# Order of the first loads, and of the first K chunks, in a gated mix of two linear-attention blocks

## The chip, the cores and the metric

The kernel runs on one core of a Trainium2 chip. The metric is device time in microseconds (us), the median of three timed runs. A core has TensorE (PE) for matmuls, VectorE (DVE), ScalarE (ACT), GpSimd (POOL) and SyncE (SP), each with an instruction queue of its own, and 16 DMA engines, which take the transfers that SP and ACT issue.

## The reference

x has 2048 rows of 640, there are two blocks A and B with 32 heads of 20, and only A's x is used.

```python
g = sigmoid((x * gate_w).sum(-1))
for each block:
    q, k, v = split(x @ wqkv)               # 640 -> 3 x 640, by heads
    phi = lambda t: where(t > 0, t + 1, exp(t)) + 1e-6
    pq, pk = phi(q), phi(k)
    kv = pk^T v ; z = sum over rows of pk   # by head
    o = (pq kv) / (pq z + 1e-6)
    y = o @ wo
out = g * a + (1 - g) * b
```

## The kernel before

x is held twice: as rows in `xn` (128 partitions, 16 chunks of 128 rows, 640) and transposed in `xT` (128 partitions, 5 column blocks, 2048). The first four row chunks of `xT` are made by PE: `x_transpose` transposes the five 128x128 blocks of a chunk into a PSUM tile `xt` and VectorE copies them out, in one piece or in two (blocks 0 and 1, then 2 to 4; `cuts`). The other twelve chunks come by transposing DMAs from HBM, issued by SP (L135).

A K chunk is x @ wk for 128 rows: ten matmuls of 320 columns, five column blocks c by two halves (`k_mm`, L207), summed in one of four PSUM slots of two banks each. `k_done` then calls `phi`: an exp on ACT (L197), a `tensor_scalar` on VectorE (min with 1, plus epsilon, L200) and a `scalar_tensor_tensor` on VectorE (x + 1, max, L204), which writes `pk`. Q products have weights as the stationary operand and 512 rows of xT as the moving one (L256, L267).

The program starts like this. SP and ACT issue the first loads: four chunks of x (160 KB each, `load_x`, L117) and the five row blocks of wkA (160 KB each, `load_wk`, L120). After them SP issues wqA (800 KB, L131) and the transposing loads. PE runs seven warm-up matmuls on constants (L164) and then `k_first`, whose order is written out by hand under `manual_schedule`: every engine takes its instructions in the order in which they are written. `k_first` handles chunks 0 to 3. Before, chunks 0 and 1 are transposed, their blocks c = 0 and 1 are multiplied, chunk 2 is transposed, block 2 of chunks 0 and 1 follows, then blocks 0 to 2 of chunk 2, the transposes of chunk 3, blocks 3 and 4 of chunks 0, 1 and 2 with `k_done` after each, and at last chunk 3 as a whole. Then come Q products and further K chunks, then block A's sums, block B, and the output products.

DMAs signal landing on eight semaphores in turn. A ninth transfer is issued only when the first one on its semaphore has landed; before, that is wqA.

Of the kernel before, what the change touches and what calls it, by code (L numbers as in the profile page):

```python
# [8 lines left out]
P = 128  # L9
# [7 lines left out]
DT = D // P  # L17
# [3 lines left out]
HB = 512  # L21
# [12 lines left out]
def kernel(  # L34
# [11 lines left out]
    nc = tc.nc  # L46
# [13 lines left out]
    def ps_raw(name, slot=None):  # L60

        if slot is None:
            slot = turn[0]
            turn[0] = (slot + 1) % 4
        return psum.tile([P, 4 * HB], BF16, tag=f"ps{slot}", name=name)

    def ps(name, slot=None):

        return ps_raw(name, slot).bitcast(FP32).rearrange("p (b n) -> p b n", b=2)

    xT = persist.tile([P, DT, S], BF16, name="xT")
# [44 lines left out]
    def load_x(eng, lo, hi):  # L116
        eng.dma_start(out=xn[:, lo:hi, :], in_=xb0[:, lo:hi, :])  # L117

    def load_wk(eng, lo, hi):
        eng.dma_start(out=wk[0][:, lo:hi, :], in_=wq_dram[0][:, lo:hi, D:2 * D])  # L120

    load_x(nc.sync, 0, 1)
    load_x(nc.scalar, 1, 2)
    load_wk(nc.sync, 0, 1)
    load_wk(nc.scalar, 1, 2)
    load_wk(nc.sync, 2, 3)
    load_x(nc.scalar, 2, 3)
    load_wk(nc.sync, 3, DT)
    load_x(nc.scalar, 3, 4)
    wq[0] = wpool.tile([P, DT, D], BF16, tag="wq", name="wqA")  # L130
    nc.sync.dma_start(out=wq[0][:], in_=wq_dram[0][:, :, 0:D])  # L131
    gcol = persist.tile([P, DT], BF16, name="gcol")
    for n in range(1, NB):
        for c in range(DT):
            nc.sync.dma_start_transpose(  # L135
                out=xT[:, c, n * HB:(n + 1) * HB], in_=x2[n * HB:(n + 1) * HB, c * P:(c + 1) * P]
# [4 lines left out]
    for r in range(4):  # L141
# [3 lines left out]
        out=spread[:].rearrange("p (h t) -> p h t", t=TW), in_=I4[:, :, None].to_broadcast([P, H, TW])  # L145
    )
    nc.gpsimd.memset(maskE[:], 1.0)
    for sign, base in ((1, 0), (-1, Dh - 1)):
        nc.gpsimd.affine_select(
            out=maskE[:], in_=maskE[:], pattern=[[-sign * Dh, WB[0] // Dh], [0, Dh]],  # L150
# [3 lines left out]
    for sign, base in ((1, 0), (-1, TW - 1)):  # L154
        nc.gpsimd.affine_select(
            out=headE[:], in_=headE[:], pattern=[[-sign * TW, H]],
# [25 lines left out]
            nc.scalar.activation(out=ge[b][:], in_=pt[:, 1, :], func=ACT.Exp, scale=(-1.0, 1.0)[b])  # L182
            nc.vector.tensor_scalar(ge[b][:], ge[b][:], 1.0, 1e30, op0=ALU.add, op1=ALU.min)

    def x_transpose(i, slot, eng, cuts=(0, DT)):
        pt = ps_raw("xt", slot)
        for c in range(DT):
            nc.tensor.transpose(out=pt[:, c * P:(c + 1) * P], in_=xn[:, i, c * P:(c + 1) * P], identity=ident[:])
        copy = nc.scalar.copy if eng == "act" else nc.vector.tensor_copy
        src = pt[:, 0:D].rearrange("p (c n) -> p c n", c=DT)  # L190
        for lo, hi in zip(cuts, cuts[1:]):
            copy(out=xT[:, lo:hi, i * P:(i + 1) * P], in_=src[:, lo:hi])  # L192

    def phi(dst, src, n, lifted=False):

        e = work.tile([P, 2, n], BF16, tag="e", name="e", bufs=3)
        nc.scalar.activation(out=e[:], in_=src, func=ACT.Exp)  # L197
        if lifted:
            nc.scalar.activation(out=dst, in_=src, func=ACT.Identity, bias=lift[:])
        nc.vector.tensor_scalar(e[:], e[:], 1.0, EPS, op0=ALU.min, op1=ALU.add)  # L200
        if lifted:
            nc.vector.tensor_tensor(out=dst, in0=dst, in1=e[:], op=ALU.max)
            return
        nc.vector.scalar_tensor_tensor(out=dst, in0=src, scalar=1.0 + EPS, in1=e[:], op0=ALU.add, op1=ALU.max)  # L204

    def k_mm(b, i, c, pt, hf):
        nc.tensor.matmul(  # L207
            pt[:, hf, 0:HF], lhsT=xT[:, c, i * P:(i + 1) * P], rhs=wk[b][:, c, hf * HF:(hf + 1) * HF],
            start=(c == 0), stop=(c == DT - 1),
        )  # L210

    def k_done(b, i, pt):
        phi(pk[:, i, :].rearrange("p (b n) -> p b n", b=2), pt[:, :, 0:HF], HF)

    def k_chunk(b, i, slot=None):
        pt = ps(f"k{'AB'[b]}", slot)
        for hf in range(2):
            for c in range(DT):
                k_mm(b, i, c, pt, hf)
        k_done(b, i, pt)  # L220

    def k_first():

        pts = [ps("kA", (2 + i) % 4) for i in (0, 1)]

        def part(i, cs):
            for c in cs:
                for hf in range(2):
                    k_mm(0, i, c, pts[i], hf)

        for i in range(2):
            x_transpose(i, i, "dve", (0, 2, DT))
        for i in range(2):
            part(i, (0, 1))
        x_transpose(2, 0, "dve", (0, 2, DT))
        for i in range(2):
            part(i, (2,))
        pts.append(ps("kA", 1))
        part(2, (0, 1, 2))
        x_transpose(3, 0, "dve")  # L240
        for i in range(3):
            part(i, (3, 4))
            k_done(0, i, pts[i])
        k_chunk(0, 3, 0)

    def mixed(t, m):
# [426 lines left out]
    with tc.manual_schedule():  # L673
        k_first()
# [11 lines left out]
    for n in range(1, NB):  # L686
        nc.sync.dma_start(
            out=xn[:, n * CB:(n + 1) * CB, :], in_=x2[n * HB:(n + 1) * HB, :].rearrange("(q p) d -> p q d", p=P)
# [8 lines left out]
    def bank(pool, name, n=1):  # L697
        return pool.tile([P, HB] if n == 1 else [P, n, HB], FP32, tag=name, name=name)

    with tc.manual_schedule():  # L700
# [30 lines left out]
        part = [slice(n * RB, (n + 1) * RB) for n in range(4)]  # L731
# [17 lines left out]
        with late_pool("single") as single:  # L749
# [6 lines left out]
            pts = [bank(single, f"s4{hf}")[:, 0:HF] for hf in range(2)]  # L756
# [20 lines left out]
        later = {2: (2, (1, 2)), 3: (2, (4,)), 4: (3, (2, 4))}  # L777
# [55 lines left out]
```

## Time and profile before

| what | value |
|---|---|
| timed runs | 189.77, 189.83 and 190.37 us; median 189.83 |
| profiled execution, its span (first to last instruction) | 188.1 us; the median of the runs is 1.7 us above it |
| busy: PE, DVE, ACT, POOL | 182.7 us (97%), 150.3 (80%), 75.0 (40%), 2.8 (2%) |
| granted TensorE clock | 1.000 |
| DMA | 15.63 MB, mean 83 GB/s; 319 to 387 GB/s from 3 to 8 us |
| first transposes; first k matmul; first q matmul | at 3.90, 4.77 and 11.72 us |

The profile is of one execution, and its times count from the start of its span. It gives no time of that execution other than the span. A timeline row names its start, how long the group lasted, the engine, the line, the operation with the tile written and the tiles read, the number of instructions, and in brackets the idle time before it and what ended that. A matmul's duration is that of one result; the next one starts earlier, so rates are read from starts. Rows with PEld are weight loads, those with ACTq and SPq are issues from these queues. "DMA to landing" is the time from issue until the last part of a transfer has signalled.

### The profile page before, as it was taken

The page shows a single profiled execution, that of the slowest core. Times are in us where ns is not written, and L with a number is a line of the kernel's source. Part 1 is how long each engine was busy: PE and PEld are TensorE (multiplying, and loading weights), DVE is VectorE, ACT ScalarE, POOL GpSimd, SP SyncE. Part 2 cuts the span into 40 slices and gives each one's busy share as a digit, 9 for nine tenths or more (in the row PEclk, how much of TensorE's full clock was granted, in tenths as well). Part 3 has the DMA queues.
Part 4 walks back from the last instruction along what each step waited for, and adds up shares of the span by engine and source line. Part 5 has one row for each costly group of instructions (what it writes and reads, how often), then busy time and mean ns, then how long its engine had stood idle before and what let it go on. Part 6 is the DMA issues. An engine that isn't in the chain of part 4 may idle for free.

```text
span 188.1 us, 3574 instructions
## 1 busy us (share of the span) xinstructions
PE 182.7 (97%) x1460; PEld 123.5 (66%) x1465; DVE 150.3 (80%) x244; ACT 75.0 (40%) x106; POOL 2.8 (2%) x17
## 2 busy tenths in 40 slices
PE   8899999999999999999999999999999999999992
PEld 3566657755577677877765555576778776777772
DVE  1378968899998999799889997739699989787553
ACT  2055446457942501367674577422401611111110
POOL 6000000000000000000000000000000000000000
PEclk9999999999999999999999999999999999999999
DMA  5975447992140000011115000000543003211222
GB/s 184 320 124 94 105 84 250 360 249 87 16 164 0 3 0 0 3 33 33 54 44 189 2 0 0 3 0 0 178 112 62 3 3 112 97 70 56 87 71 71
DMA packets 19802, 15.63 MB, mean 83 GB/s; under 512 B 9546, under 2 KB 19658, under 8 KB 19786
## 3 DMA queue, kind: packets, MB, share of 16 engines
q1 hardware_dynamic: 18922, 14.59, 29.0%
q10 hardware_dynamic: 864, 0.82, 1.3%
q8 instruction: 11, 0.18, 0.4%
q14 instruction: 5, 0.04, 0.1%
HBM read 10.00 MB, written 3.44 MB: 71 GB/s over the span
## 4 chain that ended last, share of the span: by engine, by line
PE 93%; DMA 3%; DVE 1%; ACTq 0%; issue 0%; ACT 0%; DVEq 0%
PE gs L325 16%; PE kB L207 12%; PE qB L256 11%; PE kA L207 11%; PE qA L256 7%; PE ox L563 6%; PE oy L563 5%; PE oz L563 5%; PE qA L267 5%; DMA xn<-in_A_x_dram 3%; PE ow L563 3%; PE gB L298 2%; PE gA L298 2%; DVE osb L568 1%; PE mA L456 1%; PE mid L417 1%
## 5 line engine op out<-in xcount | busy, mean ns | idle before, releaser
L207 PEld LDWEIGHTS <-xT 128*128 128x128 bf16 x320 | 31.0, 98 | 12.4 <-DVE xT L192 0.5
L200 DVE TENSOR_SCALAR e<-e 128x640 bf16<-128x640 bf16 (+1 forms) x52 | 18.7, 360 | 6.3 <-ACT e L197 5.7
L207 PE MATMUL kB<-wkB,xT 128*128 128x320 bf16 x160 | 23.0, 299 | 0.0
L207 PE MATMUL kA<-wkA,xT 128*128 128x320 bf16 x160 | 22.6, 299 | 0.1
L256 PE MATMUL qB<-xT,wqB 128*128 128x512 bf16 x98 | 21.7, 379 | 0.1
L197 ACT ACTIVATE e<-kB 128x640 bf16<-128x640 f32 x16 | 11.3, 704 | 18.8 <-PE kB L207 17.5
L256 PEld LDWEIGHTS <-wqB 128*128 128x128 bf16 x100 | 11.7, 117 | 9.8 <-issue 0.2
L197 ACT ACTIVATE e<-kA 128x640 bf16<-128x640 f32 x16 | 11.0, 704 | 13.3 <-PE kA L207 13.3
L204 DVE SCALAR_TENSOR_TENSOR pk<-kA,e 128x640 bf16<-128x640 f32 x16 | 13.2, 825 | 1.7
L204 DVE SCALAR_TENSOR_TENSOR pk<-kB,e 128x640 bf16<-128x640 f32 x16 | 13.2, 825 | 1.7
L197 ACT ACTIVATE e<-qA 128x1024 bf16<-128x1024 f32 x10 | 10.2, 1023 | 9.3 <-PE qA L267 3.7
L197 ACT ACTIVATE e<-qB 128x1024 bf16<-128x1024 f32 x10 | 10.2, 1023 | 8.7 <-PE qB L256 8.4
L256 PE MATMUL qA<-xT,wqA 128*128 128x512 bf16 x59 | 13.2, 379 | 0.1
L607 ACT COPY u<-ox 128x320 f32<-128x320 f32 x8 | 3.4, 425 | 21.9 <-PE ox L563 21.9
L325 PEld LDWEIGHTS <-S 128*128 128x128 bf16 x96 | 9.4, 98 | 3.6
L325 PEld LDWEIGHTS <-xn 128*128 128x128 bf16 x96 | 9.1, 98 | 4.0 <-issue 0.4
L256 PEld LDWEIGHTS <-wqA 128*128 128x128 bf16 x60 | 7.0, 117 | 5.8
L563 PEld LDWEIGHTS <-xT 128*128 128x128 bf16 x85 | 8.0, 98 | 3.1 <-DVE xT L502 0.2
L591 ACT COPY p1s<-ox 128x320 f32<-128x320 f32 x8 | 3.4, 426 | 16.6 <-PE ox L563 16.6
L563 PEld LDWEIGHTS <-pqTA 128*128 128x128 bf16 x85 | 7.9, 98 | 2.9 <-issue 0.2
L563 PEld LDWEIGHTS <-pqTB 128*128 128x128 bf16 x80 | 7.8, 98 | 3.0
L325 PE MATMUL gs<-pk,xn 128*128 128x320 bf16 x64 | 9.4, 300 | 0.0
(124 smaller groups left out, 285.2 us busy)
## 6 DMA issues: line engine op xcount, KB each, us to landing
out_dram<-osb SPq DMA_DIRECT2D x14, 160.0 KB, 1.8
xn<-in_A_x_dram SPq DMA_DIRECT2D x3, 640.0 KB, 6.8
wqA<-in_A_wqkv_dram SPq DMA_DIRECT2D x1, 800.0 KB, 7.3
wvA<-in_A_wqkv_dram SPq DMA_DIRECT2D x1, 800.0 KB, 11.8
wkB<-in_B_wqkv_dram SPq DMA_DIRECT2D x1, 800.0 KB, 6.3
wqB<-in_B_wqkv_dram SPq DMA_DIRECT2D x1, 800.0 KB, 4.8
MA<-ma_dram SPq DMA_DIRECT2D x1, 800.0 KB, 4.3
wvB<-in_B_wqkv_dram SPq DMA_DIRECT2D x1, 800.0 KB, 5.7
```

The source lines that it names most:

```text
L197: nc.scalar.activation(out=e[:], in_=src, func=ACT.Exp)
L200: nc.vector.tensor_scalar(e[:], e[:], 1.0, EPS, op0=ALU.min, op1=ALU.add)
L204: nc.vector.scalar_tensor_tensor(out=dst, in0=src, scalar=1.0 + EPS, in1=e[:], op0=ALU.add, op1=ALU.max)
L207: nc.tensor.matmul(pt[:, hf, 0:HF], lhsT=xT[:, c, i * P:(i + 1) * P], rhs=wk[b][:, c, hf * HF:(hf + 1) * HF], start=(c == 0), stop=(c == D ...
L256: nc.tensor.matmul(pt[:, u, :], lhsT=mixed(wq[b][:, c, :], m), rhs=xT[:, c, n * HB:(n + 1) * HB], start=(c == 0), stop=(c == DT - 1),)
L267: nc.tensor.matmul(pt[:, u, :], lhsT=mixed(wq[b][:, c, :], m + u), rhs=xT[:, c, n * HB:(n + 1) * HB], start=(c == 0), stop=(c == DT - 1),)
L298: nc.tensor.matmul(pt[:, hf, 0:HF], lhsT=xn[:, i, c * P:(c + 1) * P], rhs=pk[:, i, hf * HF:(hf + 1) * HF], start=(i == 0), stop=(i == ST - 1),
L325: nc.tensor.matmul(pt[:, n, 0:HF], lhsT=left[:, i, n * P:(n + 1) * P], rhs=right[:, i, :], start=(first and i == 0), stop=(i == hc - 1), s ...
L417: nc.tensor.matmul(pt[:KG, hf, j * KG:(j + 1) * KG], lhsT=wv[b][:, c, (4 * hf + j) * KG:(4 * hf + j + 1) * KG], rhs=GT[hf][:, c, j * KG:(j ...
L563: nc.tensor.matmul(dst, lhsT=left[:, c, r0:r0 + P], rhs=right[:, c, :], start=(first and c == 0), stop=(c == DT - 1), skip_group_check=not ...
L591: nc.scalar.copy(out=self.p1s[:], in_=self.at("x"))
L607: nc.scalar.copy(out=self.u2[:], in_=self.at("x"))
```

## The change

The first loads are issued in another order and from other queues. Before, SP: x0, wk0, wk2, wk3 and wk4 in one; ACT: x1, wk1, x2, x3. After, SP: x0, x1, wk2, wk4, x3; ACT: wk0, wk1, wk3, x2. There are nine transfers instead of eight, so x3 is now the one that waits for an earlier landing (wk0's) on the shared semaphore.

In `k_first`, chunks 0 and 1 are transposed as before; then blocks 0 to 3 are multiplied for both chunks in turn; then chunk 2 is transposed; then block 4 of chunks 0 and 1 follows, with `k_done` of each; then chunk 2 with all its blocks; then the transposes of chunk 3, `k_done` of chunk 2, and chunk 3. Chunk 2's copy to xT is one instruction instead of two, and the transposes of chunks 2 and 3 write the two halves of one PSUM tile. On VectorE the copy of chunk 3 now stands behind the `phi` instructions of chunks 0 and 1 and ahead of those of chunk 2; before it stood ahead of all of them.

```diff
     load_x(nc.sync, 0, 1)
-    load_x(nc.scalar, 1, 2)
-    load_wk(nc.sync, 0, 1)
+    load_wk(nc.scalar, 0, 1)
+    load_x(nc.sync, 1, 2)
     load_wk(nc.scalar, 1, 2)
     load_wk(nc.sync, 2, 3)
+    load_wk(nc.scalar, 3, 4)
+    load_wk(nc.sync, 4, DT)
     load_x(nc.scalar, 2, 3)
-    load_wk(nc.sync, 3, DT)
-    load_x(nc.scalar, 3, 4)
+    load_x(nc.sync, 3, 4)
...
-    def x_transpose(i, slot, eng, cuts=(0, DT)):
-        pt = ps_raw("xt", slot)
+    def x_transpose(i, pt, cuts=(0, DT)):
...
         for i in range(2):
-            x_transpose(i, i, "dve", (0, 2, DT))
+            x_transpose(i, ps_raw("xt", i), (0, 2, DT))
+        for c in range(DT - 1):
+            for i in range(2):
+                part(i, (c,))
+        later = ps_raw("xt", 0)
+        x_transpose(2, later[:, 0:2 * HB])
         for i in range(2):
-            part(i, (0, 1))
-        x_transpose(2, 0, "dve", (0, 2, DT))
-        for i in range(2):
-            part(i, (2,))
+            part(i, (DT - 1,))
+            k_done(0, i, pts[i])
         pts.append(ps("kA", 1))
-        part(2, (0, 1, 2))
-        x_transpose(3, 0, "dve")
-        for i in range(3):
-            part(i, (3, 4))
-            k_done(0, i, pts[i])
+        part(2, range(DT))
+        x_transpose(3, later[:, 2 * HB:])
+        k_done(0, 2, pts[2])
         k_chunk(0, 3, 0)
```

More of the change, by code (lines that the diff above doesn't have):

```diff
@@ L183, in gate_pass @@
             nc.vector.tensor_scalar(ge[b][:], ge[b][:], 1.0, 1e30, op0=ALU.add, op1=ALU.min)
-    def x_transpose(i, slot, eng, cuts=(0, DT)):
-        pt = ps_raw("xt", slot)
+    def x_transpose(i, pt, cuts=(0, DT)):
         for c in range(DT):
             nc.tensor.transpose(out=pt[:, c * P:(c + 1) * P], in_=xn[:, i, c * P:(c + 1) * P], identity=ident[:])
-        copy = nc.scalar.copy if eng == "act" else nc.vector.tensor_copy
         src = pt[:, 0:D].rearrange("p (c n) -> p c n", c=DT)
         for lo, hi in zip(cuts, cuts[1:]):
-            copy(out=xT[:, lo:hi, i * P:(i + 1) * P], in_=src[:, lo:hi])
+            nc.vector.tensor_copy(out=xT[:, lo:hi, i * P:(i + 1) * P], in_=src[:, lo:hi])
     def phi(dst, src, n, lifted=False):
```

## Prediction

> **What bounds the kernel now.** I read the chain of waits first, for the engine that sets the end.
>
> ```profile
> PE 93%; DMA 3%; DVE 1%; ACTq 0%; issue 0%; ACT 0%; DVEq 0%
> ```
>
> The chain is PE from end to end, with one piece of DMA. Busy time by stretches then tells whether a delay could be taken back: from 12 to 182 us PE is busy for 169.7 of 170 us (3.95 of 4.00, 5.95 of 6.00, 17.95 of 18.00, and so on), and after 182 us come only the last products, additions and stores. So the start of the first q product is the clock of everything behind it: what the change adds or saves ahead of it comes out at the end one for one.
>
> Next the chain inside the first 15 us:
>
> ```profile
> 1.73 5.02 DMA xn<-in_A_x_dram
> 6.75 0.05 issue
> 6.79 0.45 PE xt L188 x5
> 7.25 1.37 PE kA L207 x10
> 8.62 0.28 PE xt L188 x5
> 8.90 2.99 PE kA L207 x22
> ```
>
> The DMA piece is the third x chunk: issued by ACT at 1.73, landed at 6.75, its transposes at 6.79. The PE timeline shows the hole, and the rates I shall need:
>
> ```profile
> 0.84 3.06 PE L164 MATMUL warm<-const-bfloat16-1.0 128*128 128x512 bf16 x7 [0.84 <-PEq L817]
> 3.90 0.73 PE L188 MATMUL xt<-ident,xn 128*128 128x128 bf16 x10
> 4.77 1.25 PE L207 MATMUL kA<-wkA,xT 128*128 128x320 bf16 x8
> 6.79 0.45 PE L188 MATMUL xt<-ident,xn 128*128 128x128 bf16 x5 [0.77 <-DMA xn<-in_A_x_dram]
> 8.74 3.15 PE L207 MATMUL kA<-wkA,xT 128*128 128x320 bf16 x22
> 11.72 4.48 PE L267 MATMUL qA<-xT,wqA 128*128 128x512 bf16 x19
> ```
>
> A k matmul takes (11.72-8.74)/22 = 0.1355 us of PE's time, its result 0.30 us; a transpose takes 0.28/5 = 0.056. From 3.90 to 11.72 lie 20 transposes (1.12) and 40 k matmuls (5.42), 6.54 us of work in 7.82: 1.28 us idle. Two holes make it: 0.31 before 4.77 (the first copy of xT) and 6.79-(4.77+8x0.1355) = 0.94 before 6.79. That 0.94 is all there is to win from the loads, and not all can be won: wqA is issued at 4.07 and lands 7.3 us later, at 11.4, where q starts its weight load at 11.59.
>
> Last, VectorE, which the change reorders:
>
> ```profile
> 4.39 1.02 DVE L192 COPY xT<-xt 128x256 bf16<-128x256 bf16 x4 [2.91 <-PE xt L188]
> 7.28 0.56 DVE L192 COPY xT<-xt 128x256 bf16<-128x256 bf16 x2 [1.87 <-PE xt L188]
> 8.94 0.49 DVE L192 COPY xT<-xt 128x640 bf16<-128x640 bf16 x1 [1.10 <-PE xt L188]
> 10.22 0.33 DVE L200 TENSOR_SCALAR e<-e 128x640 bf16<-128x640 bf16 x1 [0.79 <-ACT e L197]
> 10.67 0.82 DVE L204 SCALAR_TENSOR_TENSOR pk<-kA,e 128x640 bf16<-128x640 f32 x1
> 11.41 0.32 DVE L200 TENSOR_SCALAR e<-e 128x640 bf16<-128x640 bf16 x1
> 11.83 0.82 DVE L204 SCALAR_TENSOR_TENSOR pk<-kA,e 128x640 bf16<-128x640 f32 x1
> 12.57 0.32 DVE L200 TENSOR_SCALAR e<-e 128x640 bf16<-128x640 bf16 x1
> ```
>
> All xT copies stand ahead of the first phi. The copy of the fourth chunk (8.94) is done at 9.43, under matmuls that do not need it. Each phi then holds VectorE for 1.16 us (10.22, 11.41, 12.57).
>
> **Part 1, the loads.** Issue to landing of each in the DMA view: SP's first (x0) 3.0 and ACT's first (x1) 3.2, so 3.8 and 4.0; the second ones (wk0, wk1) 3.5 and 3.7, so 4.75 and 4.95; the third ones (wk2, x2) 4.8 and 5.0, so 6.5 and 6.75; the fourth ones (wk rows 3 and 4 as one 320 KB transfer, x3) 5.7 and 5.4, so 7.8 and 7.6. From 3 to 8 us the DMA share is 0.95 to 1.08 with 319 to 387 GB/s, so it is place in the queue that sets a landing, not the queue's name. I give the new order the old landings place by place: x0 3.8, wk0 4.0, x1 4.75, wk1 4.95, wk2 6.5, wk3 6.75, x2 7.6, wk4 7.4 to 7.8. x3 is now SP's fifth and the ninth transfer on eight semaphores; its issue waits for wk0's landing (4.0), as wqA's waited for x1's, so wqA and the fifteen transposing loads go out some 0.4 us later (one SP issue, 0.39 to 0.44). That is hidden: wqA would land near 11.8 and is wanted, below, at 13.3; the first transposed block is wanted at 16.04 plus the shift. If PE came early it would not be hidden.
>
> **Part 2, the start on PE.** The transposes of x0 still run at 3.90 to 4.18 (the warm-up matmuls end there anyway). x1 was there at 4.0; now PE waits until 4.75+0.05 = 4.80: 0.62 idle. Its transposes end at 5.08, chunk 0 has two matmuls to 5.35, and chunk 1 needs the first copy of x1: transposes to copy 0.49 (3.90 to 4.39), copy 0.28, copy to weight load 0.07, to matmul 0.03, so 5.67: 0.32 idle. Then c0 of chunk 1 and c1 of both, six matmuls, to 6.48, c2 from wk2 at 6.55 (0.07 idle) to 7.09, c3 to 7.63 (wk3 is there). x2 at 7.65: transposes to S = 7.93. The hole of 0.94 is gone, but 0.62+0.32+0.07+0.02 = 1.03 us of new ones replace it and the old 0.31.
>
> **Part 3, the end of the k start, counted from S.** c4 for chunks 0 and 1: four matmuls to S+0.54. Chunk 2 needs all of x2's copy, now one piece (0.49): copy from S+0.21, weight load S+0.77, matmul S+0.80, so 0.26 idle. Ten matmuls end at S+2.155, x3's transposes at S+2.435. Before, this copy lay under fourteen matmuls and more. Now the next instruction on PE is chunk 3, which needs it, and on VectorE it is issued behind the phis of chunks 0 and 1. Those run so: the last c4 matmul of chunk 0 ends at S+0.435, ACT's exp at S+0.465 (as 9.45 to 9.48 before), tensor_scalar 0.74 later at S+1.205 (9.48 to 10.22), scalar_tensor_tensor 0.45 later at S+1.655 (10.22 to 10.67), next tensor_scalar 0.74 later at S+2.395, its partner 0.42 later at S+2.815, and the copy 0.74 later at S+3.555. It ends at S+4.045, chunk 3 starts at S+4.145: PE idle for 1.71 us. Were the copy taken as soon as the transposes allow (S+2.155+0.49 = S+2.645), chunk 3 would start at S+3.235 and PE idle 0.80; that is the low bound of this term, 0.91 less. I take 1.71: VectorE's rows of before stand in program order, and the third tensor_scalar came at 12.57 although the three exps were done at 9.48+1.90 = 11.38.
> [...]
>
> **The sum.** Idle between the first transposes and q: before 0.31+0.94 = 1.25; after 1.03+0.26+1.71 = 3.00. The work is the same 40 matmuls and 20 transposes, and one VectorE copy less costs nothing (its chunk is off the path except for the 0.26 counted). Difference +1.75; by absolute times, S+5.50 = 13.43 against 11.72, +1.71. I take +1.7. Against the profiled execution that is a span of 189.8 for 188.1; the median of the runs, 189.83, is 1.7 above the span and I keep that distance: 191.5 us.
>
> **The bounds.** Low: if x1, wk2 and x2 all land as early as the matmuls can use them, PE sets S alone: 5.85 (where the first eight matmuls end before) + 8x0.1355 + 0.28 = 7.2, which makes the difference +1.0; with late loads but the low bound of the copy, 0.91 less, it is +0.8: 190.6. Both at once are a rival. High: one load late by what a third landing lost against a second (1.75 from second to third, 0.95 from first to second, so 0.8), or timed runs of before in which the 0.94 hole was small: +2.6, so 192.5.
>
> **The rivals.**
> *The weights of q decide in both kernels.* wqA landed 0.2 us ahead of need; landings here vary from 3.0 to 7.4 us. If in timed executions it lands after 13.4, that is 9.3 us after issue and not 7.3, q starts there in either kernel and the late copy costs nothing; only the 0.4 of the later issue is left: 189.8 to 190.2. Against it: in the trace PE starts q without a wait, and the runs agree within 0.6 us. 4%.
> *The loads win and the copy passes.* With S at 7.2 and the copy of x3 taken as soon as it is ready, idle is 0.31+0.26+0.80 = 1.37 against 1.25: 189.9, no change. For it: the 0.94 hole does go, and part of a load's lag may be chance. Against it: x1 is now second on its queue, and the copy must overtake two phis on VectorE. 3%. Even this is no gain: PE has nothing to do between x3's transposes and chunk 3, so a faster kernel would need something that I do not see; 2% for that.
> *The clock falls in the new holes.* The warm-up's 512-column matmuls start 0.42 apart, q's later 0.22 apart; after the 0.94 us hole of before the k matmuls kept 0.137, so that hole cost no clock. One of 1.71 us is not shown. If it halved the rate for as long as the warm-up took (3.06 us), half of that, 1.5 us, comes on top: 193.0. 4%.
> [...]
>
> **How the numbers follow.** The forecast, slower by about 1.7 us, has 87%, the rivals 4, 3 and 4%, the unseen gain 2%. A measurement of this kernel can tell 0.3%, 0.57 us, from no change. Slower by more: 0.91 (forecast and clock); within: 0.07; faster: 0.02. The range 190.6 to 192.5 leaves out the rivals (11%), the unseen gain and the ends of the forecast.
>
> **What would show it.** Right: PE idle ahead of x1's transposes until about 4.8, no hole before x2's; VectorE with two tensor_scalar and scalar_tensor_tensor pairs ahead of the last 128x640 copy; chunk 3 waiting on that copy for 1.5 to 1.9 us; q near 13.4; PE closed after that. Wrong: that copy starting within 0.5 us of x3's transposes, q's first matmul waiting for wqA, or any k matmul at 0.27 instead of 0.135.

## The result, and the profile after

The changed kernel takes 191.09 us (median of 6 runs, 190.85 to 191.50), the kernel before 189.96 (6 runs, 189.61 to 190.56): ratio 1.0057, 95% interval 1.0038 to 1.0076, so 1.1 us slower. A second comparison gave 1.0071 (1.0041 to 1.0101). The forecast was 191.5, slower.

The profiled execution took 191.50 us with a span of 189.6, so 1.9 us lie around the span; it was the slowest of the six. Its PE timeline answers to the one shown of before:

```profile
3.80 1.49 PE L188 MATMUL xt<-ident,xn 128*128 128x128 bf16 x10
5.08 3.10 PE L206 MATMUL kA<-wkA,xT 128*128 128x320 bf16 x16
8.02 0.44 PE L188 MATMUL xt<-ident,xn 128*128 128x128 bf16 x5
8.30 2.28 PE L206 MATMUL kA<-wkA,xT 128*128 128x320 bf16 x14
10.42 0.44 PE L188 MATMUL xt<-ident,xn 128*128 128x128 bf16 x5
12.39 1.53 PE L206 MATMUL kA<-wkA,xT 128*128 128x320 bf16 x10 [1.53 <-DVE xT L191]
13.76 4.48 PE L267 MATMUL qA<-xT,wqA 128*128 128x512 bf16 x20
```

The hole ahead of chunk 2's transposes is gone; a larger one stands ahead of chunk 3, from 10.42+0.28 = 10.70 to 12.39, and its releaser is the copy on L191. q starts at 13.76 for 11.72. VectorE's timeline shows why that copy is late:

```profile
8.50 0.49 DVE L191 COPY xT<-xt 128x640 bf16<-128x640 bf16 x1 [2.61 <-PE xt L188]
9.51 0.33 DVE L199 TENSOR_SCALAR e<-e 128x640 bf16<-128x640 bf16 x1 [0.52 <-ACT e L196]
9.95 0.82 DVE L203 SCALAR_TENSOR_TENSOR pk<-kA,e 128x640 bf16<-128x640 f32 x1
10.69 0.32 DVE L199 TENSOR_SCALAR e<-e 128x640 bf16<-128x640 bf16 x1
11.11 0.82 DVE L203 SCALAR_TENSOR_TENSOR pk<-kA,e 128x640 bf16<-128x640 f32 x1
11.85 0.48 DVE L191 COPY xT<-xt 128x640 bf16<-128x640 bf16 x1
```

The transposes of chunk 3 began at 10.42; with 0.49 from transposes to copy, it could have started at 10.91. It starts at 11.85, with no idle time before it: the two phis ahead of it filled VectorE. The chain of waits now runs through ACT's exp and these phis (pieces in order of time):

```profile
8.46 0.29 PE kA L206 x2
8.77 0.71 ACT e L196
10.78 0.24 DVE e L199
11.11 0.82 DVE pk L203
11.94 0.41 DVE xT L191
12.39 1.53 PE kA L206 x10
```

Yet q is 2.04 us later and the span only 1.5 longer. The rest is at the other end of the program, in the DMA view of the last stores, before and then after:

```profile
out_dram<-osb ACTq DMA_DIRECT2D x2, 80.0 KB, 2.0
out_dram<-osb SPq DMA_DIRECT2D x2, 80.0 KB, 1.8
```

```profile
out_dram<-osb ACTq DMA_DIRECT2D x2, 80.0 KB, 1.6
out_dram<-osb SPq DMA_DIRECT2D x2, 80.0 KB, 1.6
```

The last VectorE additions, before and then after:

```profile
184.50 0.61 DVE L568 TENSOR_TENSOR osb<-oz,u 128x160 bf16<-128x160 f32 x2
```

```profile
186.54 0.61 DVE L568 TENSOR_TENSOR osb<-oz,u 128x160 bf16<-128x160 f32 x2
```

From q's start to these additions both kernels take the same (184.50-11.72 = 172.78, 186.54-13.76 = 172.78), but the last four stores land sooner, and from q's start to the end of the span it is 175.8 instead of 176.4.

### The profile page after: what moved, and what is told of

Read it like the earlier page. It is cut to its first block, busy times and chain, and to the rows that moved or that the text cites. A ratio compares the mean times of both kernels' runs of the same rounds, so it can differ in the third digit from the quotient of the medians.

```text
span 189.6 us, 3578 instructions
## 1 busy us (share of the span) xinstructions
PE 184.3 (97%) x1465; PEld 124.1 (65%) x1465; DVE 150.1 (79%) x243; ACT 75.1 (40%) x106; POOL 2.8 (1%) x17
## 4 chain that ended last, share of the span: by engine, by line
PE 93%; DVE 3%; DMA 2%; ACT 1%; issue 0%; SPq 0%; DVEq 0%; ACTq 0%
PE gs L325 16%; PE kB L206 11%; PE qB L256 11%; PE kA L206 11%; PE qA L256 7%; PE ox L563 6%; PE oy L563 5%; PE oz L563 5%; PE qA L267 5%; PE ow L563 3%; PE gB L298 2%; PE gA L298 2%; DMA xn<-in_A_x_dram 2%; DVE osb L568 1%; DVE pk L203 1%; PE mA L456 1%
## 5 line engine op out<-in xcount | busy, mean ns | idle before, releaser
L206 PE MATMUL kA<-wkA,xT 128*128 128x320 bf16 x160 | 23.5, 305 | 1.6 <-DVE xT L191 1.5
L203 DVE SCALAR_TENSOR_TENSOR pqTB<-qB,e 128x1024 bf16<-128x1024 f32 x7 | 8.6, 1225 | 1.1 <-PE qB L256 0.5
```

The costliest lines, as they stand in the source:

```text
L206: nc.tensor.matmul(pt[:, hf, 0:HF], lhsT=xT[:, c, i * P:(i + 1) * P], rhs=wk[b][:, c, hf * HF:(hf + 1) * HF], start=(c == 0), stop=(c == D ...
```

## The experiments

Theory 1: VectorE's order and the uncovered copies make the kernel slower. Theory 2: the order of the loads does. Theory 3: a TensorE clock that rises later does. Ratios are to the kernel before, run beside each on the same chip; its medians there were 190.17 to 190.26 us.

**Phis behind the copy (e1).** Loads and PE order as in the changed kernel:

```diff
         for i in range(2):
             part(i, (DT - 1,))
-            k_done(0, i, pts[i])
...
         x_transpose(3, later[:, 2 * HB:])
-        k_done(0, 2, pts[2])
+        for i in range(3):
+            k_done(0, i, pts[i])
```

> The changed kernel with the phis of chunks 0 and 1 issued behind the copy of chunk 3 on VectorE; loads and PE order unchanged. If the copy's place behind two phis costs 0.9 us (theory 1), the copy starts about 0.5 us after x3's transposes begin, PE idles 0.7 to 0.8 us before chunk 3 instead of 1.5, and the time falls to about 190.2 us. If the later landing of x1 makes the loss (theory 2), or a TensorE clock that rises later (theory 3), it stays near 191.1.

190.07 us, 0.9994 (0.9976 to 1.0013). The loss is gone.

```profile
9.76 0.44 PE L188 MATMUL xt<-ident,xn 128*128 128x128 bf16 x5
10.79 1.53 PE L206 MATMUL kA<-wkA,xT 128*128 128x320 bf16 x10 [0.59 <-DVE xT L191]
```

PE idles from 10.04 to 10.79, 0.75 us against 1.69: the place behind two phis costs 0.94 us. What is left is the wait for the copy itself, with no other work for PE under it.

**Both transposes together (e2).** `x_transpose(3, ...)` directly behind `x_transpose(2, ...)`.

> The changed kernel with the transposes and the copy of chunk 3 right behind those of chunk 2, so ahead of block 4 and of the phis on PE and on VectorE; loads unchanged. Theory 1: both idle stretches behind S (0.26 and 1.5 to 1.7 us) are gone, q starts 1.8 us earlier unless wqA's landing near 11.4 us holds it: 189.2 to 189.7 us, so 0.3 to 0.7 below the kernel before. Theory 2: x1's lateness stays in full and the time is 190.5 or more. Theory 3: about 191, since the PE has no fewer holes ahead of the clock's rise.

189.73 us, 0.9975 (0.9959 to 0.9991): 0.5 us faster than before, within theory 1's 0.3 to 0.7. A new wait took some of the gain:

```profile
7.34 0.44 PE L188 MATMUL xt<-ident,xn 128*128 128x128 bf16 x5
8.37 0.44 PE L188 MATMUL xt<-ident,xn 128*128 128x128 bf16 x5 [0.58 <-DVE xT L191]
```

Chunk 3's transposes wait for chunk 2's copy out of `xt`, which ends at 8.31. The two chunks use the two halves of one PSUM tile, so this reads as the framework holding the write to one half until the other half is read; a version with two tiles was not run.

**The loads alone (e3).** The kernel before, with the new list of loads.

> The kernel before with the new order of loads alone. x1 lands at 4.6 instead of 4.0 and x2, wanted after blocks 0 and 1, as ACT's fourth at 7.1 to 7.6 instead of 6.75. By the landings: x2's transposes at 7.2 to 7.65 instead of 6.79, so 190.4 to 190.8 us. If the loads are what makes the changed kernel slow (theory 2) it is 191.1 or more; if they cost nothing by themselves it is 190.0.

189.66 us, 0.9965 (0.9946 to 0.9984): faster, which none of the expectations allowed. x2 did not land at 7.1 to 7.6: its transposes run at 7.00.

```profile
5.09 2.07 PE L208 MATMUL kA<-wkA,xT 128*128 128x320 bf16 x8
7.00 0.44 PE L189 MATMUL xt<-ident,xn 128*128 128x128 bf16 x5
12.03 4.51 PE L268 MATMUL qA<-xT,wqA 128*128 128x512 bf16 x20
```

PE takes these transposes as soon as it is done with the eight matmuls ahead. q's weight load waits 0.3 us for wqA, PE itself 0.1. Theory 2 is out: by themselves the loads make the kernel 0.6 us faster. In the trace that gain lies at the end of the program (below), for q starts 0.1 to 0.3 us later than in the two traces of before.

**The order alone (e4).** The new `k_first`, with the loads of before.

> The new order of the K chunks with the loads of before, where wk3 and wk4 come as one 320 KB transfer at 7.8 us. Block 3 then waits for it: S about 8.6 to 8.7 instead of 7.9 to 8.3, and the copy behind the phis costs the same 1.5 to 1.7 us: 191.8 to 192.4 us (theory 1). If the loads make the loss (theory 2), about 190.

192.78 us, 1.0127 (1.0097 to 1.0157), above the range expected: S is 8.96, not 8.6 to 8.7. PE idles 1.10 us for wk3 and wk4 (block 3 at 8.14 instead of 7.04), and again 13.06-(11.07+0.28) = 1.71 us for chunk 3's copy. The new order does need the new loads, and is slow with either.

**x1 first (e5).** The changed kernel with wk0 and x1 exchanged on the two queues.

> The changed kernel with x1 first on ACT's queue and wk0 second on SP's (x0, wk0, wk2, wk4, x3 on SP; x1, wk1, wk3, x2 on ACT). If x1's second place costs the 0.6 to 0.9 us of idle that the prediction gave it, S falls by up to that, bounded by x2's landing at 6.8 to 7.1 us: 0.3 to 0.6 us below the changed kernel, so 190.5 to 190.8. If the landings of wk2, wk3 and x2 bind anyway, no change: 191.1.

191.26 us, 1.0047 (1.0027 to 1.0068), not told apart from the changed kernel; the 190.5 to 190.8 did not come. The wait for x1 is gone (k matmuls from 4.91), but chunk 2's transposes still start only at 7.69: the sixteen k matmuls ahead of them take 2.78 us, against 2.47 in the changed kernel's second trace (e13 below) and 2.94 in its first. How fast PE runs in these microseconds, which changes from execution to execution, outweighs 0.3 us of earlier start in single traces; the timed runs show no gain from it.

**Copies ahead of the phis (e7).** Transposes of chunk 3 between block 4 and chunk 2, then the phis:

```diff
         for i in range(2):
             part(i, (DT - 1,))
+        x_transpose(3, later[:, 2 * HB:])
+        for i in range(2):
             k_done(0, i, pts[i])
         pts.append(ps("kA", 1))
         part(2, range(DT))
-        x_transpose(3, later[:, 2 * HB:])
         k_done(0, 2, pts[2])
```

> The changed kernel with the transposes of chunk 3 behind block 4 of chunks 0 and 1 and ahead of chunk 2, and both copies ahead of all phis; loads unchanged. PE's idle behind S is then about 0.2 us (x3's transposes behind x2's copy), q starts near 11.4 us or when wqA lands (10.6 to 12.0 in the traces so far): 189.2 to 189.6 us, below the kernel before by 0.4 to 0.8. If the VectorE order were not what made the changed kernel slow, it would be near 191.

189.66 us, 0.9966 (0.9953 to 0.9979). Chunks 2 and 3 now run without a hole, and the next bound is seen:

```profile
8.72 2.88 PE L206 MATMUL kA<-wkA,xT 128*128 128x320 bf16 x20
11.87 4.51 PE L268 MATMUL qA<-xT,wqA 128*128 128x512 bf16 x20 [0.27 <-DVE e L199]
```

VectorE is named there because its semaphore came last by the profile; q's weight load waited 0.6 us for wqA, as the waits say:

```profile
PEld L268 <- DMA wqA<-in_A_wqkv_dram: 0.6, 1, 0.6
```

**The last stores (e8, e10, e11, e12).** The changed kernel issues one first transfer more on SP. e8 is the kernel before with

```diff
-    load_wk(nc.sync, 3, DT)
+    load_wk(nc.sync, 3, 4)
+    load_wk(nc.sync, 4, DT)
```

> The kernel before with one edit: wk3 and wk4 as two loads on SP instead of one, so nine first transfers and every later transfer one place further on the semaphores. In the traces the last stores of both kernels with eight loads land 1.8 to 2.0 us after their issue, of all four kernels with nine 1.6 us. If the number of transfers sets that, the last stores land in 1.6 us here and the time is 0.3 to 0.5 us below before; if the new order of the loads sets it, they land in 1.8 to 2.0 us and the time is that of before.

189.40 us, 0.9952 (0.9938 to 0.9966); the last stores land in 1.6 us. The gain, 0.9 us (0.6 to 1.2 by the interval), is above the 0.3 to 0.5 expected; the trace shows 0.5 to 0.7 of it at the end (table below), with q at 11.70 as before.

e10 splits wqA (blocks 0 to 2, 3 and 4) instead, behind all first loads:

> The kernel before with wqA as two loads on SP (row blocks 0 to 2, then 3 and 4), so one more transfer on SP and the first eight loads untouched. If one more transfer on SP is what makes the last stores land sooner, they land in 1.6 us and the time is 0.4 to 0.6 us below before; if the order or size of the first loads does it, 1.8 to 2.1 us and no change.

189.34 us, 0.9969 (0.9944 to 0.9993); 1.6 us again. So the first loads' order and size are not needed for it.

e11 splits x3 on ACT into two loads of 320 columns:

> The kernel before with x3 as two loads of 320 columns on ACT, so one more transfer on ACT and none on SP. If the number of transfers of both queues together counts (the turn on the eight semaphores), the last stores land in 1.6 us as with one more on SP: 0.4 to 0.6 us below before. If SP's own number counts, they land in 1.8 to 2.1 us: no change.

190.74 us, 1.0052 (1.0025 to 1.0080); 2.0 and 1.9 us. One transfer more on ACT does not help the end, and at the head the split costs: x2 and x3 came late (waits of 0.80 and 0.42 us), q at 12.88.

e12 has both splits of e8 and e10:

> The kernel before with both splits on SP, wk3 from wk4 and wqA in two: two more transfers. If more transfers on SP are better as such, the last stores land in 1.6 us or less; if it is a matter of odd and even, or of one place in a ring, they land in 1.8 to 2.1 us again and the time is that of before, 0.4 to 0.9 us above the kernel with nine loads.

189.57 us, 0.9985 (0.9963 to 1.0006); the stores land in 1.6 us, so it is not odd and even. In time it is not told apart from before.

**The two kernels once more.** e9 is before, for a second trace:

> The kernel before, unchanged, for a second trace. If the late x2 (6.75 us) was one engine's accident, x2 lands at 5.7 to 6.2 us here, the hole before its transposes is under 0.4 us and wqA's landing starts q; if it belongs to the kernel, the hole is 0.8 to 1.0 us again. The last stores land in 1.8 to 2.0 us if that is the kernel's own.

```profile
4.91 1.98 PE L207 MATMUL kA<-wkA,xT 128*128 128x320 bf16 x8
6.96 0.45 PE L188 MATMUL xt<-ident,xn 128*128 128x128 bf16 x5
11.89 4.48 PE L267 MATMUL qA<-xT,wqA 128*128 128x512 bf16 x20
```

x2 is late again (issued at 1.73, 5.2 us to landing), so that is no accident, but there is hardly a hole: the eight matmuls ahead take 1.98 us, where they took 1.25, and PE is busy while x2 is on its way. One run, 190.4 us; last stores 2.1 and 1.9 us.

e13 is the changed kernel:

> The changed kernel, unchanged, for a second trace, since the first one was of its slowest execution (191.50 us against a median of 191.09) and its clock rose late (half rate until 6.6 us). If the prediction's sum holds for a common execution, q starts at 13.2 to 13.6 us, the idle ahead of chunk 3 is 1.5 to 1.7 us again, and the last stores land in 1.6 us; time 1.0 to 1.2 us above before.

191.18 us, 1.0071 as above.

```profile
4.91 2.62 PE L206 MATMUL kA<-wkA,xT 128*128 128x320 bf16 x16
7.38 0.44 PE L188 MATMUL xt<-ident,xn 128*128 128x128 bf16 x5
9.77 0.44 PE L188 MATMUL xt<-ident,xn 128*128 128x128 bf16 x5
11.75 1.53 PE L206 MATMUL kA<-wkA,xT 128*128 128x320 bf16 x10 [1.54 <-DVE xT L191]
13.12 4.48 PE L267 MATMUL qA<-xT,wqA 128*128 128x512 bf16 x20
```

q is 0.3 us below the forecast's 13.43 here and 0.3 above it in the first trace; the idle ahead of chunk 3 is 11.75-10.05 = 1.70. Theory 3 is judged here by the rate of the first k matmuls, which start 0.27 us apart at first and 0.136 later; the profile's row of the granted clock reads 1.00 in all these microseconds, so that a clock is behind the rate is the author's reading. The rate rose early in the first trace of before (eight k matmuls in 1.25 us) and late in that of after (sixteen in 3.10), and the other way round in the second pair (1.98 in e9, 2.62 in e13), where the changed kernel is still the slower one: 13.12-11.89 = 1.23 us at q. So theory 3 explains the spread, 0.6 us of q between two traces of one kernel, and not the difference.

All traces together, sorted by what SP issues more than in the kernel before:

| kernel | SP's transfers more | last stores, ACT and SP, us to landing | q start | span | from q to the end |
|---|---|---|---|---|---|
| before | 0 | 2.0, 1.8 | 11.72 | 188.1 | 176.4 |
| before again (e9) | 0 | 2.1, 1.9 | 11.89 | 188.5 | 176.6 |
| order alone (e4) | 0 | 1.9, 1.8 | 14.43 | 190.8 | 176.4 |
| x3 in two on ACT (e11) | 0 | 2.0, 1.9 | 12.88 | 189.3 | 176.4 |
| after | 1 | 1.6, 1.6 | 13.76 | 189.6 | 175.8 |
| after again (e13) | 1 | 1.6, 1.6 | 13.12 | 189.0 | 175.9 |
| phis behind the copy (e1) | 1 | 1.6, 1.6 | 12.16 | 188.0 | 175.8 |
| transposes together (e2) | 1 | 1.6, 1.6 | 11.90 | 187.8 | 175.9 |
| loads alone (e3) | 1 | 1.6, 1.6 | 12.03 | 188.0 | 176.0 |
| x1 first (e5) | 1 | 1.6, 1.6 | 13.43 | 189.3 | 175.9 |
| copies ahead of phis (e7) | 1 | 1.6, 1.6 | 11.87 | 187.8 | 175.9 |
| before, nine loads (e8) | 1 | 1.6, 1.6 | 11.70 | 187.6 | 175.9 |
| wqA in two (e10) | 1 | 1.6, 1.6 | 11.53 | 187.4 | 175.9 |
| ten loads (e12) | 2 | 1.6, 1.6 | 11.73 | 187.7 | 176.0 |

Everything between q and the end falls into two groups, 176.4 to 176.6 and 175.8 to 176.0, and SP's number of transfers is what parts them. From q to the last additions all fourteen take 172.76 to 172.93, so the groups part behind these.

The traces have a likely cause, in packets that the DMA view lists under "instruction" (queue q14). One of them, 8 KB, falls into the last microseconds of every trace. In the kernel before it starts at 185.53, right behind SP's issue of its last store (185.14 to 185.47), takes 0.65 us and runs among the packets of the last stores. In the kernel after it starts at 184.76, 1.4 us ahead of SP's last two issues, and is over before they begin. First before, from 185.4 to 186.3 us, then after, from 184.5 to 185.3:

```profile
q14 instruction: 1, 0.01, 4.5%
```

```profile
q14 instruction: 1, 0.01, 3.0%
```

All the traces part in this way: in the four with the late stores the packet starts 0.04 to 0.06 us behind SP's last issue, 1.0 us after the start of the last additions; in the other ten it starts ahead of SP's last two issues, 0.9 to 1.9 us before these additions. And what is late in the kernel before is one small part of each store. 1.9 us after the start of the last additions (186.40 before, 188.44 after) this is still to move:

```profile
DMA packets 10, 0.01 MB, mean 13 GB/s; under 512 B 2, under 2 KB 10, under 8 KB 10
```

```profile
DMA packets 0, 0.00 MB, mean 0 GB/s; under 512 B 0, under 2 KB 0, under 8 KB 0
```

Nine of the ten are of SP's last store. A store has 144 packets; spread evenly over the 16 DMA engines that would be nine each, so what is left is as much as one engine's share. The author's reading is that the instruction packet holds up one DMA engine, and that SP's number of instructions (91 in the four, 92 or 93 in the ten) sets when that packet runs. This is argued and not shown: the trace does not name a packet's engine, and no run moved the packet and nothing else.

## Why the prediction was right, and where it was off

Point by point:

- *The copy of chunk 3 behind two phis, PE idle 1.71 us.* Measured 1.69, 1.70 and 1.71 (after, e13, e4). Of that, 0.91 was put down to the order on VectorE and 0.80 to the copy itself; e1 gave 0.94 and 0.75. VectorE kept the program's order, as its rows of before do: a copy that could have started at 10.91 waited until 11.85. Counted from S, the first trace follows part 3 step by step: exp at S+0.47, the copy at S+3.55, chunk 3 at S+4.09, q at S+5.46, against S+0.465, 3.555, 4.145 and 5.50.
- *Chunk 2's copy, 0.26.* Measured 10.42-(8.30+14x0.1355) = 0.22.
- *The loads, place by place.* The transposes of x1 were put at 4.80 and came at 4.57 and 4.62; x2 as ACT's fourth was given the old fourth landing, 7.6, and landed near 7.1 and 6.7 (issued at 2.2, 4.9 and 4.5 us to landing). In the first trace every load from the second place on took less from issue to landing than the one in its place before (SP 3.3, 4.4 and 4.7 us for 3.5, 4.8 and 5.7; ACT 3.5, 4.6 and 4.9 for 3.7, 5.0 and 5.4); all of these are of 160 KB now, and one of those before is of 320 KB. The 0.62 and 0.32 us of idle charged to x1 came out as about 0.34 and 0.27 in e13, and not as a price: e5 took the wait away and gained nothing that can be measured.
- *S at 7.93, set by the landing of x2.* It was 8.30 and 7.65, and x2 did not set it: PE came to the transposes 0.9 and 0.7 us after x2 had landed, straight from the sixteen k matmuls ahead, some of them at the low rate (0.27 us apart). The prediction had the landings too late and PE too fast, and the two cancel in the mean of 7.98. That is luck.
- *The hole of 0.94 as all that the loads could win.* In e9 there is next to no hole, and yet chunk 2's transposes start at 6.96. The hole was the slack of an execution in which the matmuls' rate rose early (eight in 1.25 us, against 1.98 in e9), with x2's landing as the bound.
- *q at 13.43, 1.71 us late.* The traces of after have 13.76 and 13.12, mean 13.44; those of before 11.72 and 11.89, mean 11.80. That is 1.64 us: part 3 came as forecast, S by another path.
- *"What the change adds or saves ahead of it comes out at the end one for one."* This is the step that failed. It holds up to the last addition, 172.78 us behind q's start in both, but not for the stores behind it. There about 0.6 us came back (176.5 to 175.9 in the means of two traces each), for a reason that lies in the change (one more transfer on SP). 1.64-0.6 = 1.0, and 1.1 was measured (0.7 to 1.4 by the interval). With this term the forecast would have been 190.9.
- *The median 1.7 us above the span.* In the later runs, where span and time are of the same execution, the distance is 1.8 to 2.1 us (191.50 for 189.6, 190.4 for 188.5). The 1.7 set one execution's span against the median of others, and was some 0.2 us small.
- *The rivals.* wqA did not start q in the changed kernel; it does in e3 and e7, where PE would be ready for q at 11.9 and 11.4. The matmuls did not slow behind the hole of 1.7 us: the ten there take (13.76-12.39)/10 = 0.137 each. One sign that was to show the forecast wrong, a k matmul at 0.27, did appear, from 5.08 to 6.45 in the first trace, but at the start, ahead of the rise of the rate, and not behind the hole of 1.7 us.

Two small edits make kernels that beat both: one load split in two (e8, 0.9952) and the copies ahead of the phis (e7, 0.9966). Their gains cannot be added: e7 has the ninth load on SP and its shorter end already, and q's weight load waits 0.6 us for wqA there.

## What to carry to other kernels

Before a copy out of PSUM is moved, look at what stands ahead of it in its engine's queue, not only at when its input is ready: two pairs of vector instructions of 1.16 us each ahead of one 0.49 us copy made the next stage of PE 0.94 us late. Where the next PE work needs a copy at once, put other PE work between transposes and use. And when a PE-bound program is costed, cost its two ends separately: here the middle carried a shift one for one (172.76 to 172.93 us from q to the last additions in all fourteen traces), and the last stores did not (1.6 us to landing, or 1.8 to 2.1). One transfer more on SP at the start went with about 0.6 us less at the other end of the program, so look at the packets there too.

## What had not been expected of the hardware

- The last 80 KB stores land 1.6 us after issue when SP has issued one or two transfers more at the start of the program, and 1.8 to 2.1 us when it has not (ten traces against four); one transfer more on ACT does nothing. An 8 KB instruction packet lies among these stores in the four traces and ahead of SP's last two issues in the ten.
- The first k matmuls run at one of two rates (starts 0.27 or 0.136 us apart), and the change between them comes at another time in each execution of the same kernel (five transposes from 3.94 us take 0.45 already in e7, eight k matmuls from 5.09 still 2.07 in e3): eight matmuls in 1.25 us in one trace of before and in 1.98 us in the other; five transposes and their way to the copy 0.49 us there, 0.75 us (3.80 to 4.55) in the first trace of after. Between the two traces of before, where x2's landing bounds the head, chunk 2's transposes start 0.17 us apart (6.79 and 6.96); between those of after, where PE does, 0.64 us (8.02 and 7.38). No run shows what sets the time of the change.
